# Causal scores of two batches as one step of 64-wide tile products, with the key halves of every second batch exchanged

## The chip, the cores and the metric

The kernel runs on one core of a Trainium2 chip. The metric is device time in microseconds (us), from the start of the launch to its end on that core. Where a profile is spoken of, it is one further execution, recorded by the hardware profiler; its times are counted from its first instruction.

The engines are named as the profile names them: PE (TensorE, matrix products; PEld is its loading of stationary operands), DVE (VectorE), ACT (ScalarE), POOL (GpSimd), and SP, whose queue issues all DMAs here.

## The reference, cut to what matters

An mLSTM cell (4 batches, 8 heads, 768 tokens, head size 40) is followed by a feed-forward layer with exact GELU (320 to 2048 to 320) on its 3072 output rows.

```python
for t in range(S):                               # one head of one batch
    m_new  = np.maximum(f[t] + m, i[t])
    f_stab, i_stab = np.exp(f[t] + m - m_new), np.exp(i[t] - m_new)
    C = f_stab * C + i_stab * np.outer(v[t], k[t])
    n = f_stab * n + i_stab * k[t]
    y[t] = sigmoid(o[t]) * (C @ q[t]) / np.maximum(np.abs(n @ q[t]), 1.0)
    m = m_new
x = y.transpose(0, 2, 1, 3).reshape(B * S, H * D)
out = gelu(x @ w_in) @ w_out
```

## The kernel before, in words

**Chunks.** The 768 tokens are cut into six chunks of 128 (c = 0 to 5). Within a chunk the recurrence is written as causal attention: scores k·q of 128 by 128 tokens for each head, times weights exp(a[s] − M[t]) that are zero where s comes after t, times the values with a column of ones. What comes from earlier chunks is q times a carried state. A chunk has four batches (b = 0 to 3). A **step** is one piece of this for one batch, and has a letter. The feed-forward layer of chunk c runs on the PE between the cell steps of chunk c + 1.

**The steps that matter here**, for c of 2 and more:

- `M` (`mask`, L381, POOL): the tile with M for all tokens t, sent to all 128 partitions by a DMA, gets a large number where s > t.
- `W` (`weights`, L407, ACT): eight exponentials, one for each head, with the column `aT[:, c, head]` (a of the token on each partition) as bias. Masked places become 0.
- `K` and `Q` (`turn_k`, `turn_q`, L430, DVE): k and q of one batch are turned to kT and qT, 64 partitions for each of two heads. `K` also forms `vw`, the values times `ewT` (L466, POOL).
- `S` (`scores`, L479, PE; L482, DVE): for each of four head pairs p and both heads of it (`hip`), the 64 by 128 slice of kT is the stationary operand and the 64 by 128 slice of qT is the moving one. The result is 128 tokens s by 128 tokens t. The two heads of a pair use the upper and the lower 64 rows of the PE array and write to two PSUM banks. Then DVE multiplies each bank (128x512) into the weights, in place. Nothing is saved for the masked triangle: 16 products of 128 columns for two batches.
- `C` (`carry_two`, two batches at once): q times state in 64 by 64 tiles of the PE array (L531), the new state's part from k and `vw` (L538, not in the last chunk), then DVE and POOL work on the results (L547, L554, L555).
- `V` (`values`, L573, PE): for each head and each half of the tokens t, weights times values, 128 rows by 64 columns of the array. DVE adds the carried part (L581).
- `F`: one of fourteen pieces of the down product (L844, 8 matmuls each). `Y`, `X`, `R` finish a batch and hand it to the feed-forward layer.

**Where the order comes from.** It is written out by hand, in the strings `FRONT` (chunks 0 and 1) and `DOWN` (later chunks); each engine executes its instructions in that order. The part of `DOWN` around the change reads as follows for a chunk, with `Z` empty except in chunk 2:

```
M0 Z M1 W0 F L3 F B3 W1 Z Z F S0 Z S1 K2 C0 M2 Z G0 G1 G2 G3 V0 Z V1 W2 Z F Q2 K3 Q3
Y0 M3 D3 F F W3 F Z S2 S3 C2 V2 V3 F ...
```

So on the PE a pair of batches is S, S, C, V, V, and then F; on DVE it is the products of both S, the turning `K2`, and then the results of C and V. `B3` sends M of the fourth batch by DMA (L162), after the sixteen small DMAs that `L3` issues for its k and q (L145); `M3` and `W3` can only run after it.

**PSUM.** S of an even batch takes two banks of pool `ps_mm` (tag "a"), S of an odd batch both banks of pool `ps_tr`. `V` uses tag "a" as well, `C` uses `ps_h`, `F` uses `ps_mm` tag "b".

Of the kernel before, what the change touches and what calls it, by code (L numbers as in the profile page):

```python
# [9 lines left out]
F32 = mybir.dt.float32  # L10
# [4 lines left out]
OP = mybir.AluOpType  # L15

P = 128
# [10 lines left out]
FRONT = """  # L28
    I2 O0 g0 L0 P0 L1 E k1 t0 P1 P2 k7 w0 N k2 w1 O1 K L2 Q s0 O3 w2 q D k2 d P3 t1 w3 c0 L3 J v0 t2 K K y0 s1 I7 v1
    I8 O2 J g1 L4 I5 c1 K I1 I2 y1 s2 x0 t3 B4 O4 B5 g2 J x1 s3 v2 c2 L5 y2 H T0 x2 G0 v3 g3 c3 K y3 M1 J L6 J A x3  # L30
    M0 K W0 O7 K A O6 O5 J M2 W1 S0 C0 K J J T1 U U K L7 V0 K T2 J J A G2 K G1 Y0 W2 S1 K M3 C1 A J S2 J K W3 K V1 C2
    Y1 T3 J J U U S3 V2 K K J G3 J Y2 C3 X0 K V3 J K F J F K K B8 F J K F F J K F F F R0 X1 J J K F J F K X2 F J K F
    J Y3 K F R1 J F Z B9 B10 F X3 R2 Z R3 F"""
DOWN = """
    M0 Z M1 W0 F L3 F B3 W1 Z Z F S0 Z S1 K2 C0 M2 Z G0 G1 G2 G3 V0 Z V1 W2 Z F Q2 K3 Q3 Y0 M3 D3 F F W3 F Z S2 S3
    C2 V2 V3 F N F Y1 X0 R0 Y2 F F Y3 X1 R1 F X2 R2 F X3 R3 F"""


# [1 line left out]
def kernel(  # L40
# [29 lines left out]
    R = P // 2  # L70
# [30 lines left out]
    aT = const.tile([P, NCH, BH], F32, name="aT")  # L101
    ewT = const.tile([P, NCH - 1, BH], F32, name="ewT")
# [9 lines left out]
    W = {n: shared([P, H, L], F32, f"W{n}") for n in range(B - 1)}  # L112
# [9 lines left out]
    f_sb = gates.tile([BH, NCH, L], F32, name="f_sb")  # L122
    i_sb = gates.tile([BH, NCH, L], F32, name="i_sb")
    M_d = dram.tile([NCH - 1, BH, L], F32, name="M_d")

    def out_of(n):
        return ob[n % NLD].rearrange("p (h d) -> p h d", d=D)

    def load(n, first=0, end=4):

        if n >= NCH * B:
            return
        c, b = divmod(n, B)
        for src, dst in ((q, qb), (k, kb), (v, vb), (o_gate, None))[first:end]:
            nc.sync.dma_start(out=dst[turn_of(n)][:, :, 0:D] if dst else out_of(n),  # L135
                              in_=src[b, :, c * L:(c + 1) * L, :].rearrange("h p d -> p h d"))

# [12 lines left out]
    def turn_of(n):  # L150

        return n % NLD if n < 2 * B else (n - 2 * B) % NQ
# [19 lines left out]
    for t in vb:  # L172
# [15 lines left out]
    a = gates.tile([BH, NCH, L], F32, name="a")  # L188
# [7 lines left out]
    for j in range(3):  # L196
        m = slice(BH * j, BH * (j + 1))
# [17 lines left out]
    def gates_turned(*parts):  # L215

        for src, dst in parts:
            n = dst.shape[1]
            pg = ps_tr.tile([P, n, BH], F32, name="pg", tag="tr")
            for c in range(n):  # L220
                nc.tensor.transpose(pg[:, c, :], src[:, c, :], ident[0:BH, 0:BH])
            nc.vector.tensor_copy(out=dst, in_=pg)

    def gates_of(c0, c1):

        flat = lambda t: t[:, c0:c1].rearrange("p c l -> p (c l)")
# [20 lines left out]
    def decays_turned(e0, e1, g0, g1):  # L247
        e, g = slice(e0, e1), slice(g0, g1)
        gates_turned((ew[:, e], ewT[:, e]), (gg[:, g], gT[:, g]))

    def decays_last(g0, g1):
        g = slice(g0, g1)
        pd = ps_tr.tile([P, g1 - g0, BH], F32, name="pd", tag="tr")
        nc.tensor.matmul(pd.rearrange("p c n -> p (c n)"), last, gT[:, g].rearrange("p c n -> p (c n)"),
                         start=True, stop=True)
        nc.vector.tensor_copy(out=dec[:, g], in_=pd)
# [92 lines left out]
            fetch(i + NB)  # L349


    halves = (slice(0, R), slice(R, P))

    idle = [0]

    def keep_clock(steps):
# [11 lines left out]
    class Cell:  # L368
# [9 lines left out]
        def mask(self, b):  # L378

            t = Mb[self.c * B + b]  # L380
            nc.gpsimd.affine_select(out=t, in_=t, compare_op=OP.is_ge, fill=1.0e30, base=0,  # L381
                                    pattern=[[0, H], [1, L]], channel_multiplier=-1)

        def weights(self, b):

# [83 lines left out]
        def scores(self, b):  # L469
            n = self.c * B + b  # L470
            kT, qT = self.kT.pop(b), self.qT[b]

            pool, tag = (ps_tr, "tr") if self.c > 0 and b % 2 else (ps_mm, "a")
            ps = [pool.tile([P, NP, L], F32, name="ps", tag=tag) for hip in range(2)]
            unread(ps[0][:, 0, :])
            for p in range(NP):
                for hip in range(2):
                    r = halves[hip]
                    nc.tensor.matmul(ps[hip][:, p, :], kT[r, p, :], qT[r, p, :], start=True, stop=True)  # L479
            for hip in range(2):  # L480
                w = W[n].rearrange("p (m two) t -> p m two t", two=2)[:, :, hip, :]
                nc.vector.tensor_tensor(out=w, in0=ps[hip], in1=w, op=OP.mult)  # L482

        def carry(self, b):

# [419 lines left out]
    def in_turn(steps):  # L905
        todo = list(steps)
        return lambda: todo.pop(0)() if todo else None

    def cell_steps(c, letters, before=None):
        cell = Cell(c)  # L910
        cell.before = before
        return dict(zip(letters, (cell.mask, cell.weights, cell.gate, cell.turn, cell.scores, cell.carry, cell.values,
                                  cell.finish, cell.turn_y, cell.split_x, cell.load_last, cell.turn_k,
                                  cell.turn_q, cell.weigh_last, cell.carry_two,
                                  cell.last_M)))

    first_g = Hidden(False)
    n_pieces = range(len(pieces))
    steps = dict(P=fetch, L=lambda n: load(n, 0, 2), O=lambda n: load(n, 2, 4), B=load_M, E=second_gates, N=later_gates,
                 I=keep_clock, k=warm, D=lambda: decays_turned(0, 2, 0, 1), Q=lambda: decays_turned(2, NCH - 1, 1, NCH - 1),  # L920
                 d=lambda: decays_last(0, 1), q=lambda: decays_last(1, NCH - 1),
                 A=in_turn(first_up_steps(0)), U=in_turn(first_up_steps(1)), F=in_turn(first_down_steps(first_g)),
                 K=in_turn(lambda i=i: conv_one(i) for i in n_pieces), H=products_begin,
                 J=in_turn(lambda i=i: conv_two(i) for i in n_pieces), Z=split_weight)
    steps |= cell_steps(0, "mwgtscvyx") | cell_steps(1, "MWGTSCVYXR")
    play(FRONT, steps)
    for c in range(1, NCH):
        g, later, steps = Hidden(True), [], {}
        if c + 1 < NCH:
            steps = cell_steps(c + 1, "MWGTScVYXRLKQDCB", g)  # L930
        up(g, weight_sum(1) + weight_sum(2) + weight_sum(3) if c == 1 else [], [lambda b=b: (steps["K"](b), steps["Q"](b)) for b in range(2)] if steps else [])
        if c == 1:
            later = weight_sum(4)
        products, late = down_steps(c, g)
        steps |= dict(F=in_turn(products), Z=in_turn(later), N=late)
        play(DOWN if c + 1 < NCH else "F " * 14, steps)
# [30 lines left out]
```

## Time and profile before

| | |
|---|---|
| median of 3 runs | 485.5 us (485.18 to 485.93) |
| the profiled execution's own time | 484.47 us |
| its span, first to last instruction | 482.7 us |
| PE clock granted in it | 1.00 |
| PE, share of the span that a matmul is in flight | 98% |
| DVE / ACT / POOL busy | 72% / 46% / 14% |
| L479, scores, 64x128 products | 384 records, first at 15.4 us, last at 400.1 us |
| L482, DVE products on 128x512 | 48 of them, 0.68 us each |

The program holds one matrix product as one instruction, and the trace shows two records for each fp32 product (both passes over the stationary operand): 16 products are "x32". A record's duration includes the way through the array, so records overlap; what a step costs is the distance between the starts of its first record and of the next step's first record. In the chain of waits the lines show these distances; there times are up to 0.1 us later than in the timeline, because the chain hands over at modelled ends.

### The profile page before, as it was taken

How to read it: one execution, taken by the hardware profiler on the slowest of the kernel's cores; microseconds unless marked ns; L12 is line 12 of the kernel's file. 1: busy time of each engine (PE TensorE's matmuls, PEld its weight loads, DVE VectorE, ACT ScalarE, POOL GpSimd, SP SyncE). 2: the span in 40 equal slices, each digit the busy share in tenths (PEclk: the TensorE clock that was granted, in tenths of full speed). 3: DMA queues.
4: the chain of work that ended last, by engine and by line, in shares of the span. 5: the costliest groups of instructions: out<-in, count | busy, mean ns of one | idle time of the engine just before them, and what ended most of it. 6: DMA issues, size and time to landing. Idle time of an engine off the chain costs nothing.

```text
span 482.7 us, 11369 instructions
## 1 busy us (share of the span) xinstructions
PE 473.8 (98%) x4484; PEld 413.6 (86%) x4484; DVE 346.4 (72%) x744; ACT 222.3 (46%) x477; POOL 69.5 (14%) x108
## 2 busy tenths in 40 slices
PE   7999999999999999999999999999999999999997
PEld 7788888877777999977999977999977899977997
DVE  7899699898979997747498757498857397724321
ACT  6977999844632941112951113961103852112300
POOL 3001200001000234200144200145000212000000
PEclk9999999999999999999999999999999999999999
DMA  9998955379320365921264922265921250100001
GB/s 174 202 220 180 208 145 140 90 184 218 104 27 7 36 126 76 206 50 22 31 117 72 216 50 25 29 127 75 205 49 22 32 90 3 47 9 0 1 1 54
DMA packets 168021, 44.28 MB, mean 92 GB/s; under 512 B 154176, under 2 KB 161504, under 8 KB 167968
## 3 DMA queue, kind: packets, MB, share of 16 engines
q1 hardware_dynamic: 167968, 43.56, 46.4%
q8 instruction: 35, 0.57, 0.5%
q14 instruction: 18, 0.15, 0.1%
HBM read 39.52 MB, written 4.01 MB: 90 GB/s over the span
## 4 chain that ended last, share of the span: by engine, by line
PE 91%; DVE 4%; SPq 1%; ACT 1%; DMA 1%; issue 1%; DVEq 0%
PE po L844 32%; PE pu L768 21%; PE po L821 7%; PE pu L713 6%; PE pu L779 6%; PE ph L573 5%; PE ps L479 5%; PE pf L531 2%; PE pu L719 2%; PE px L608 2%; PE pf L538 1%; SPq L135 1%; PE pt L453 1%; ACT g L783 1%; PE pf L498 1%; DMA ob<-in_o_gate_dram 1%
## 5 line engine op out<-in xcount | busy, mean ns | idle before, releaser
L844 PE MATMUL po<-w_out,g 128*128 128x160 f32 x640 | 91.2, 300 | 0.0
L844 PEld LDWEIGHTS po<-w_out,g 128*128 128x128 f32 x640 | 87.8, 190 | 1.8 <-ACT g L783 1.8
L783 ACT ACTIVATE g<-pu 128x512 f32<-128x512 f32 x80 | 40.8, 616 | 53.5 <-PE pu L779 53.3
L844 PE MATMUL po<-w_sums,sums 128*128 128x160 f32 x320 | 47.2, 302 | 0.0
L844 PEld LDWEIGHTS po<-w_sums,sums 128*128 128x128 f32 x320 | 44.2, 190 | 0.4
L618 ACT ACTIVATE x_hi<-px 128x384 fp32r<-128x384 f32 x20 | 9.8, 489 | 70.6 <-PE px L608 70.6
L768 PE MATMUL pu<-x_hi,w_in_hi 128*128 128x512 f32 x160 | 41.7, 402 | 0.0
L700 DVE TENSOR_TENSOR sums<-g 128x512 f32<-128x512 f32 x20 | 13.8, 689 | 38.6 <-ACT g L783 38.6
L768 PE MATMUL pu<-x_lo,w_in_lo 128*128 128x512 f32 x160 | 40.7, 396 | 0.0
L407 ACT ACTIVATE W<-W,aT 128x128 f32<-128x128 f32 x128 | 39.1, 389 | 0.4 <-POOL W L381 0.2
L482 DVE TENSOR_TENSOR W<-ps,W 128x512 f32<-128x512 f32 x40 | 25.5, 685 | 15.9 <-ACT W L407 10.9
L768 PEld LDWEIGHTS pu<-x_hi,w_in_hi 128*128 128x128 f32 x160 | 28.5, 188 | 9.4 <-ACT g L783 4.1
L768 PEld LDWEIGHTS pu<-x_lo,w_in_lo 128*128 128x128 f32 x160 | 30.1, 188 | 7.2
L821 PE MATMUL po<-w_out,g 128*128 128x320 f32 x128 | 35.3, 434 | 0.0
L857 DVE TENSOR_TENSOR o_sb<-po,o_sb 128x320 f32<-128x320 f32 (+1 forms) x27 | 12.6, 465 | 28.9 <-PE po L844 24.8
L821 PEld LDWEIGHTS po<-w_out,g 128*128 128x128 f32 x128 | 24.0, 190 | 9.8 <-DVE w_out L348 0.2
L768 PE MATMUL pu<-x_all,w_in_mid 128*128 128x512 f32 x80 | 31.7, 396 | 0.1
L783 ACT ACT_TABLE_LOAD x5 | 6.4, 1283 | 55.1 <-DMA blocks<-in_k_dram 27.5
L768 PE MATMUL pu<-x_all,w_mid 128*128 128x512 f32 x80 | 31.7, 396 | 0.0
L419 POOL MEMSET g<- 32x1024 f32 x8 | 7.6, 944 | 155.8 <-ACT W L407 155.6
L713 PE MATMUL pu<-first_x,w_in 128*128 128x256 f32 x128 | 28.9, 382 | 0.0
L381 POOL TENSOR_SCALAR_AFFINE_SELECT W<-W 128x1024 f32<-128x1024 f32 x16 | 18.1, 1137 | 67.3 <-DMA W<-M_d 58.9
(180 smaller groups left out, 907.8 us busy)
## 6 DMA issues: line engine op xcount, KB each, us to landing
W<-M_d SPq DMA_DIRECT2D x16, 512.0 KB, 5.7
bits<-in_moe_w_in_dram SPq DMA_DIRECT2D x20, 256.0 KB, 4.1
bits<-in_moe_w_out_dram SPq DMA_DIRECT2D x16, 320.0 KB, 3.6
ob<-in_o_gate_dram SPq DMA_DIRECT2D x24, 160.0 KB, 3.9
out_dram<-o_sb SPq DMA_DIRECT2D x24, 160.0 KB, 1.9
vb<-in_v_dram SPq DMA_DIRECT2D x22, 160.0 KB, 5.1
kb<-in_k_dram SPq DMA_DIRECT2D x22, 160.0 KB, 4.8
g<-M_d SPq DMA_DIRECT2D x4, 512.0 KB, 4.2
```

The costliest lines, as they stand in the source:

```text
L381: nc.gpsimd.affine_select(out=t, in_=t, compare_op=OP.is_ge, fill=1.0e30, base=0, pattern=[[0, H], [1, L]], channel_multiplier=-1)
L407: nc.scalar.activation(out=W[n][:, h, :], in_=src, func=AF.Exp, scale=-1.0, bias=aT[:, self.c, r:r + 1])
L479: nc.tensor.matmul(ps[hip][:, p, :], kT[r, p, :], qT[r, p, :], start=True, stop=True)
L482: nc.vector.tensor_tensor(out=w, in0=ps[hip], in1=w, op=OP.mult)
L573: nc.tensor.matmul(ph[r, h, :], Pm[:, h, r], vb[turn_of(n)][:, h, :], start=True, stop=True)
L700: nc.vector.tensor_tensor(out=s1, in0=a21, in1=a22, op=OP.add)
L713: nc.tensor.matmul(banks[-1][e][:, i - i0, :], in_tile(i, x)[:, e, i % 2 * P:(i % 2 + 1) * P], first_x[:, x, t0:t1], start=(x == 0 and i = ...
L768: nc.tensor.matmul(pus[i][e], w[k][:, e, i * P:(i + 1) * P], x[:, k, :], start=(n == 0 and k == 0), stop=False, skip_group_check=True)
L779: nc.tensor.matmul(pu[e], w[r, i // 2, i % 2 * P:(i % 2 + 1) * P], x[r, NX, :], start=False, stop=(n == 2), skip_group_check=True)
L783: nc.scalar.activation(out=g.t[:, HF * e + i, :], in_=pu[e], func=AF.Gelu, scale=4097.0)
L821: nc.tensor.matmul(po[b], g.t[:, f, b * L:(b + 1) * L], w_out[:, f, :], start=(f == 0), stop=(f == NF - 1))
L844: nc.tensor.matmul(bank[at][:, i, :], lhs(j, t), rhs(j), start=(first and i == 0 and j == 0), stop=(i == n - 1 and j == HF - 1), skip_grou ...
```

## The change

`S1` and `S3` are gone from `DOWN`, and `S` there is a new function `scores_two` for batches b and b + 1 (chunks 2 to 5; chunks 0 and 1 keep `scores`). It forms 64 by 64 tile products. The first half of the tokens s meets all 128 tokens t (x = 0); the second half of s meets only the second half of t (x = 1). The quarter with s in the second and t in the first half, all of it masked, is not computed. For one p and x, two batches and two heads make four products on four different quarters of the array. To give them four different quarters, the results of the odd batch stand in exchanged halves: its first 64 tokens s are on partitions 64 to 127.

All that is indexed by s must then be exchanged for batches 1 and 3 of chunks 2 to 5: k and v as loaded for `C` and `V` (two DMAs of 64 partitions in place of one of 128), the mask (two `affine_select`, of 64x1024 and 64x512, in place of one of 128x1024), and the columns of `aT` and `ewT`. Those are written to DRAM once (`r`, 2 DMAs, in the middle of `FRONT`) and read back exchanged (`p`, 4 DMAs, at its end). DVE multiplies each bank in two parts: the columns t of the second half on all partitions, and those of the first half on 64 partitions.

```diff
-    M0 Z M1 W0 F L3 F B3 W1 Z Z F S0 Z S1 K2 C0 M2 Z G0 G1 G2 G3 V0 Z V1 W2 Z F Q2 K3 Q3 Y0 M3 D3 F F W3 F Z S2 S3
+    M0 Z M1 W0 F L3 F B3 W1 Z Z F S0 Z K2 C0 M2 Z G0 G1 G2 G3 V0 Z V1 W2 Z F Q2 K3 Q3 Y0 M3 D3 F F W3 F Z S2
...
+    def swapped(c, b):
+
+        return c > 1 and b % 2 == 1
...
+            if dst and swapped(c, b):
+                x, to = src[b, :, c * L:(c + 1) * L, :].rearrange("h p d -> p h d"), dst[turn_of(n)][:, :, 0:D]
+                for i in range(2):
+                    nc.sync.dma_start(out=to[halves[i]], in_=x[halves[1 - i]])
+                continue
...
+    def halves_out():
+
+        for t, t_d in zip((aT, ewT), swapped_d):
+            nc.sync.dma_start(out=t_d, in_=t[:, 2:])
+
+    def halves_back():
+
+        for t, t_d in zip((aT, ewT), swapped_d):
+            to, by = [x.rearrange("p c (b h) -> p (c b) h", h=H)[:, 1::2] for x in (t[:, 2:], t_d)]
+            for i in range(2):
+                nc.sync.dma_start(out=to[halves[i]], in_=by[halves[1 - i]])
...
-            nc.gpsimd.affine_select(out=t, in_=t, compare_op=OP.is_ge, fill=1.0e30, base=0,
-                                    pattern=[[0, H], [1, L]], channel_multiplier=-1)
+            for x, base in ((t[0:R], -R), (t[R:P, :, 0:R], 0)) if swapped(self.c, b) else ((t, 0),):
+                nc.gpsimd.affine_select(out=x, in_=x, compare_op=OP.is_ge, fill=1.0e30, base=base,
+                                        pattern=[[0, H], [1, x.shape[2]]], channel_multiplier=-1)
...
+        def scores_two(self, b0):
+
+            two_b = (b0, b0 + 1)
+            ps = [[pool.tile([P, NP, L], F32, name="ps", tag=tag) for hip in range(2)] for pool, tag in ((ps_mm, "a"), (ps_tr, "tr"))]
+            kT, qT = [self.kT.pop(b) for b in two_b], [self.qT[b] for b in two_b]
+            for p in range(NP):
+                for x in range(2):
+                    t = slice(R * x, P)
+                    for i in range(2):
+                        for hip in range(2):
+                            r = halves[hip]
+                            nc.tensor.matmul(ps[i][hip][halves[x ^ i], p, t], kT[i][r, p, halves[x]], qT[i][r, p, t],
+                                             start=True, stop=True)
+            for i, b in enumerate(two_b):
+                for hip in range(2):
+                    w = W[self.c * B + b].rearrange("p (m two) t -> p m two t", two=2)[:, :, hip, :]
+                    for r, t in ((slice(0, P), halves[1]), (halves[i], halves[0])):
+                        nc.vector.tensor_tensor(out=w[r, :, t], in0=ps[i][hip][r, :, t], in1=w[r, :, t], op=OP.mult)
```

More of the change, by code (lines that the diff above doesn't have):

```diff
@@ L30 @@
     I8 O2 J g1 L4 I5 c1 K I1 I2 y1 s2 x0 t3 B4 O4 B5 g2 J x1 s3 v2 c2 L5 y2 H T0 x2 G0 v3 g3 c3 K y3 M1 J L6 J A x3
-    M0 K W0 O7 K A O6 O5 J M2 W1 S0 C0 K J J T1 U U K L7 V0 K T2 J J A G2 K G1 Y0 W2 S1 K M3 C1 A J S2 J K W3 K V1 C2
+    M0 K W0 O7 K A O6 O5 J M2 W1 S0 C0 K J J T1 U U K L7 V0 K T2 r J J A G2 K G1 Y0 W2 S1 K M3 C1 A J S2 J K W3 K V1 C2
     Y1 T3 J J U U S3 V2 K K J G3 J Y2 C3 X0 K V3 J K F J F K K B8 F J K F F J K F F F R0 X1 J J K F J F K X2 F J K F
-    J Y3 K F R1 J F Z B9 B10 F X3 R2 Z R3 F"""
+    J Y3 K F R1 J F Z B9 B10 F X3 R2 Z R3 F p"""
 DOWN = """
-    M0 Z M1 W0 F L3 F B3 W1 Z Z F S0 Z S1 K2 C0 M2 Z G0 G1 G2 G3 V0 Z V1 W2 Z F Q2 K3 Q3 Y0 M3 D3 F F W3 F Z S2 S3
+    M0 Z M1 W0 F L3 F B3 W1 Z Z F S0 Z K2 C0 M2 Z G0 G1 G2 G3 V0 Z V1 W2 Z F Q2 K3 Q3 Y0 M3 D3 F F W3 F Z S2
     C2 V2 V3 F N F Y1 X0 R0 Y2 F F Y3 X1 R1 F X2 R2 F X3 R3 F"""
@@ L124 @@
     M_d = dram.tile([NCH - 1, BH, L], F32, name="M_d")
+    swapped_d = [dram.tile([P, n, BH], F32, name=f"swapped{n}") for n in (NCH - 2, NCH - 3)]
     def out_of(n):
         return ob[n % NLD].rearrange("p (h d) -> p h d", d=D)
+    halves = (slice(0, R), slice(R, P))
+    def swapped(c, b):
+        return c > 1 and b % 2 == 1
     def load(n, first=0, end=4):
@@ L349, in conv_two @@
             fetch(i + NB)
-    halves = (slice(0, R), slice(R, P))
     idle = [0]
@@ L914, in cell_steps @@
                                   cell.turn_q, cell.weigh_last, cell.carry_two,
-                                  cell.last_M)))
+                                  cell.last_M, cell.scores_two)))
     first_g = Hidden(False)
@@ L920 @@
                  I=keep_clock, k=warm, D=lambda: decays_turned(0, 2, 0, 1), Q=lambda: decays_turned(2, NCH - 1, 1, NCH - 1),
-                 d=lambda: decays_last(0, 1), q=lambda: decays_last(1, NCH - 1),
+                 d=lambda: decays_last(0, 1), q=lambda: decays_last(1, NCH - 1), r=halves_out, p=halves_back,
                  A=in_turn(first_up_steps(0)), U=in_turn(first_up_steps(1)), F=in_turn(first_down_steps(first_g)),
@@ L929 @@
         if c + 1 < NCH:
-            steps = cell_steps(c + 1, "MWGTScVYXRLKQDCB", g)
+            steps = cell_steps(c + 1, "MWGTscVYXRLKQDCBS", g)
         up(g, weight_sum(1) + weight_sum(2) + weight_sum(3) if c == 1 else [], [lambda b=b: (steps["K"](b), steps["Q"](b)) for b in range(2)] if steps else [])
```

## The prediction

> **What bounds the kernel now.** First the page's busy times, then its chain of waits. Their lines:
>
> ```profile
> PE 473.8 (98%) x4484; PEld 413.6 (86%) x4484; DVE 346.4 (72%) x744; ACT 222.3 (46%) x477; POOL 69.5 (14%) x108
> ...
> PE 91%; DVE 4%; SPq 1%; ACT 1%; DMA 1%; issue 1%; DVEq 0%
> ```
>
> PE sets the end, so a shorter PE step pays, but only if what waits behind it is ready. So I read the stage itself: the chain for the first pair of batches of chunk 3 and of chunk 5, then the DVE timeline of both.
>
> ```profile
> 238.66 1.99 PE ps L479 x32
> 240.64 1.07 PE pf L531 x64
> 241.71 1.06 PE pf L538 x32
> 242.78 1.87 PE ph L573 x64
> ...
> 384.50 1.99 PE ps L479 x32
> 386.49 1.07 PE pf L531 x64
> 387.56 2.00 PE ph L573 x64
> ```
> ```profile
> 239.88 2.49 DVE L482 TENSOR_TENSOR W<-ps,W 128x512 f32<-128x512 f32 x4 [2.84 <-ACT W L407]
> 242.28 1.41 DVE L430 STREAM_TRANSPOSE kT<-blocks 64x512 f32<-64x512 f32 x2
> ...
> 385.72 2.48 DVE L482 TENSOR_TENSOR W<-ps,W 128x512 f32<-128x512 f32 x4 [2.84 <-ACT W L407]
> 388.12 1.41 DVE L430 STREAM_TRANSPOSE kT<-blocks 64x512 f32<-64x512 f32 x2
> ```
>
> S, C, V follow each other on PE without a gap. From the start of S: F follows at 5.99 us in chunk 3 (1.99 + 1.07 + 1.06 + 1.87), at 5.05 us in chunk 5, which has no L538 (384.43 to 389.48). DVE starts 1.3 us after S does, since the even batch's scores are done half-way, and ends its four products about 3.8 us after the start (242.37). V of the odd batch starts near 4.95 us in chunk 3, 4.0 us in chunk 5. DVE's lead is 1.1 us there, 0.2 us here. That lead is the subject.
>
> The third place is the second pair of chunk 2:
>
> ```profile
> 178.86 1.09 POOL L381 TENSOR_SCALAR_AFFINE_SELECT g<-g 128x1024 f32<-128x1024 f32 x1 [4.95 <-DMA g<-M_d]
> 179.99 2.45 ACT L407 ACTIVATE g<-g,aT 128x128 f32<-128x128 f32 x8 [2.17 <-POOL g L381]
> ```
>
> S starts at 179.42; the last batch's weights are ready at 182.44, and DVE's products of it wait for that. This goes back to a DMA, not to PE.
>
> **What the Trainium skill says.** "TensorEngine Tiling (Array Packing)", Key Properties: tiles operate independently, changing the tiling mode drains the engine. The trace agrees: records of L531 start in groups of four, 7 ns apart, one group every 58 ns; from L479's last record to L531's first are 0.20 us. The same page, PSUM Bottleneck: tiling speeds up TensorE but not the emptying of PSUM, which may become the bottleneck. No run here shows that yet; it is my forecast. "TensorE: Matmul & The Clock Gate", Part 3, Measured speedup: sixteen tiles gave 10.6 times; for our four tiles the trace proves only about 2 (below). "SBUF — State Buffer", Who interferes with whom: a GpSimd instruction and a VectorE copy or tensor_scalar block each other. The trace agrees: L588 takes 0.66 us beside the POOL mask at 251.99, 0.17 us alone.
>
> **The change, part by part.**
>
> *PE, scores.* Down products give the price of a record: 128 columns of weights against 320 take 272 ns (17.43 us / 64), against 160 139 ns (8.89 / 64), so 0.83 ns a column and 5.5 ns. 128 columns: 112 ns, which is the spacing of L479's pairs of records. 64 columns: 59 ns, also the floor that L531 and L573 show with 41 columns. Four tiles at once: each head pair costs two passes of 112 and two of 59 ns, 0.34 us; four pairs 1.36, and about 0.09 for the first weights. Both S and C then use 64x64 tiles, so I drop the 0.20 us drain. D, from S to C, is 1.45 us for 1.99. The gain on PE is 0.54 x 8 = 4.3 us if nothing waits. Bounds: 1.40 without first-load cost; at worst 2.5, if four tiles stream no faster than L531 proves: 64 records in 1.07 us are 16.7 ns each against 34 ns of streaming, 2.05 at once; 32 records of 107 ns and 32 of 53 ns are 5.1 us / 2.05.
>
> *DVE, scores.* For two batches, 4 products of 512 columns become 8 of 256. Four of 512 run in 2.49 us, the last 0.68: a step of 0.60 to 0.62. Four of 164 (L547) run in 1.03, a step of 0.24 to 0.26. So 1.04 ns a column and 0.087: 0.354 for 256, the last 0.416. Eight: 2.90 us for 2.49. They no longer start half-way: every bank is completed by the last head pair. Start: last record (D − 0.06) + its 0.24 + 0.10 that DVE took after L479 (254.62 to 254.72) = D + 0.26. V of the odd batch needs all eight for its second head: D + 0.26 + 7 x 0.354 + 0.416 + 0.054 (from a DVE end to L573 at 26.99) = D + 3.21; its seven heads of 0.117 and the switch to L844 are 0.94. F follows at **D + 4.15 = 5.60 us**. PE alone would give D + 4.0 with L538, D + 3.06 without.
>
> So a pair gains 0.39 in chunks 2 to 4 and loses 0.55 in chunk 5: there the DVE products, before just hidden behind C, become the wait. What queues behind V on PE is F.
>
> *Second pairs.* DVE's later work moves back by 4.59 − 3.70 = 0.89 us (start of K2). In chunk 3 it was idle only 0.30 us before the second S's products; S comes 0.39 earlier and its products are ready 0.5 later; some 0.2 us remain as a wait. Chunk 4 had 0.86 idle: nothing. Chunk 2: its mask is now two instructions of 1.09 and about 0.64 (0.29 at 128 columns, 1.10 at 1024), so weights at 183.08, products of the odd batch till 184.6, F at 185.6 without the 0.90 us gap that the chain shows inside V at 184.83. That gap has no semaphore; I keep it: 186.5 for 186.56.
>
> *The rest, at nothing.* Masks M1: POOL is 14% busy, M1 is made a stage ahead; uncovered 0.64 each. Split loads of k and v: each SP issue takes about 0.5 us, they stand after the M of B3, and vw of chunk 3's fourth batch is ready at 254.4, 2.7 us before L538 needs it; late by 1 us it still is in time. The sixteen small loads and the M behind `L3` pass no new DMA in their chunk. `r` stands ahead of the w_out loads: two issues, about 1 us of SP, while `bits` has four buffers; uncovered 1 us, once. `p` falls into SP's idle time (129.8 to 136.4) and lands long before W1 of chunk 2 (163.95); its 1,792 packets at 21 ns over 16 engines are an estimated 2.4 us. aT is read only by later instructions.
>
> *Sum.* Chunk 2: −0.05. Chunk 3: −0.39 − 0.39 + 0.2 = −0.58. Chunk 4: −0.78. Chunk 5: +0.55 x 2 = +1.10. Together −0.3 us: 484.47, the profiled execution's own time, becomes 484.2; against the median of 485.5, one us above it, **485.2**.
>
> **The rivals.**
>
> *Slower, by DVE.* Place: the eight products before V. If halves of rows of a bank do not overlap as L547 does, a step costs its full 0.416: 7 x 0.062 = 0.43 us more in each pair but chunk 2's (7 pairs, 3.0 us): 488.2. From a step of 0.36 us on the change costs time, from 0.38 measurably. For it: DVE is at 88% in these stages. Against: L547 with a PSUM input and a broken pattern overlaps.
>
> *Slower, by PE.* Four tiles give only 2.05 streams: D = 2.5, F at 6.65; 0.66 x 5 pairs and 1.6 x 2, about +7: 492. Against: two tiles run at full rate both ways (L479 in rows, L503 in columns).
>
> *Faster.* D = 1.40, the gap of 0.90 does not return, and the mask's two parts cost no more than one: the sum's −0.3, then −0.05 x 6, −0.9 and −0.6 are −2.1: 483.4, between 483.1 and 484.2.
>
> *It doesn't do what it says.* S needs both kT at once and four banks free. DVE ends chunk 3's turning at 251.96, S starts at 253.46: 1.5 us, of which the 0.89 and 0.39 take most. If it falls short: +0.3 in each of seven pairs, 487.
>
> **How the numbers follow.** What a measurement of this kernel can tell from no change is about 0.2%, 1 us. Forecast, waits of V eat the gain: 0.52, own range 484.2 to 486.6, of which 0.05 lies below 484.5 and 0.05 above 486.5. Faster: 0.15. DVE: 0.19. PE: 0.09. Banks or kT: 0.05. So faster 0.15 + 0.05 = 0.20; within, 0.42; slower 0.33 + 0.05 = 0.38. The range 484.0 to 489.0 reaches over the DVE rival and leaves out PE's and about half of the faster one.
>
> **What would show it.** In the changed kernel's line numbers S is L518 and L524, C L573, V L615. L518 to L573 in 1.4 to 1.5 us, records in fours 112 and 59 ns apart: the PE step. L524 x8 in about 2.9 us, starting 1.7 us after S. L615 cut by a wait for DVE W, most of all in chunk 5, where F follows at 5.6 us. Busy PE falling by 4 us with the span unchanged: the forecast as a whole. I am wrong if V shows no wait, if D is above 1.7, or if anything before 160 us moves.

## The result, and the profile after

| | before | after |
|---|---|---|
| median, 13 runs each on one chip | 485.03 us (484.26 to 486.21) | 487.64 us (486.06 to 493.69) |
| ratio of the runs | 1 | 1.0060, 95% interval 1.0038 to 1.0082 |
| the profiled execution's own time, its span | 484.47, 482.7 us | 487.46, 485.6 us |

The change made the kernel slower by 0.6%, some 2.6 us; no change within 0.2% had been forecast. In 4 of the 13 runs with the change the mean granted clock lay below 0.998, and these are longer (488.7 to 493.7 us; the longest is left out of the ratio); without such runs the medians are 487.1 us with the change and 484.7 before (on the chip of e1), and the main experiments below keep their order (e7 482.7, e4 484.1, e5 484.7, e1 485.5, e10 485.7, e9 487.1).

First the page of the changed kernel, the busy times and the shares of the chain:

```profile
PE 472.1 (97%) x4740; PEld 411.4 (85%) x4740; DVE 350.0 (72%) x776; ACT 222.3 (46%) x477; POOL 76.9 (16%) x116
...
PE 68%; DVE 12%; SPq 5%; DMA 5%; ACT 5%; issue 3%; POOL 2%; DVEq 0%; ACTq 0%; POOLq 0%
```

PE is busy 1.7 us less in a span 2.9 us longer; 4 us less in an unchanged span had been forecast. It was 91% of the chain and is 68%. What it now waits for stands in the waits of PE (total us, how often, longest):

```profile
PE ph L615 <- DVE W L524: 1.9, 5, 0.5
PE ph L615 <- DMA blocks<-in_k_dram: 1.4, 1, 1.4
PE ph L615 <- DVE g L524: 1.1, 3, 0.5
...
PE px L650 <- DVE y_rest L639: 0.9, 1, 0.9
```

Three kinds: V (L615) for DVE's products, eight times; V once for what is put down to a DMA; and the last transposes X (L650) for DVE. Each in the timeline (start, duration, engine and line). For V, the first pair of chunk 5:

```profile
385.85 1.57 PE L518 MATMUL ps<-qT,kT 64*64 64x128 f32 x64
...
387.24 1.09 PE L573 MATMUL pf<-state,qT 64*64 64x41 f32 x64
387.55 3.10 DVE L524 TENSOR_TENSOR W<-ps,W 128x256 f32<-128x256 f32 x8 [3.25 <-PE ps L518]
...
389.10 1.17 PE L615 MATMUL ph<-vb,W 128*64 128x41 f32 x32 [0.28 <-DVE W L524]
...
390.79 1.02 PE L615 MATMUL ph<-vb,W 128*64 128x41 f32 x28 [0.52 <-DVE W L524]
391.73 0.43 PEld L886 LDWEIGHTS po<-w_sums,sums 128*128 128x128 f32 x3
391.74 0.54 PE L886 MATMUL po<-w_sums,sums 128*128 128x160 f32 x2
```

S to C is 1.39 us. DVE's eight end 4.79 us after S, V's second head goes on at 4.94, and F follows at 5.88. Chunk 3's second pair, V of its two batches, and chunk 4's end (DVE's finishing chain, the masks of chunk 5 on POOL, and X):

```profile
256.38 1.11 PE L615 MATMUL ph<-vb,W 128*64 128x41 f32 x32
...
258.86 1.14 PE L615 MATMUL ph<-vb,g 128*64 128x41 f32 x32 [1.37 <-DMA blocks<-in_k_dram]
```
```profile
336.12 2.08 POOL L404 TENSOR_SCALAR_AFFINE_SELECT W<-W 128x1024 f32<-128x1024 f32 x1
337.17 2.10 DVE L916 TENSOR_TENSOR g<-g,sums 128x1024 f32<-128x1024 f32 x1
...
342.27 0.49 DVE L633 TENSOR_TENSOR ob<-ob,den 128x320 f32<-128x320 f32 x1
...
343.54 1.95 POOL L404 TENSOR_SCALAR_AFFINE_SELECT W<-W 64x1024 f32<-64x1024 f32 x2 [5.34 <-DMA W<-M_d]
343.78 1.19 DVE L633 TENSOR_TENSOR ob<-ob,den 128x320 f32<-128x320 f32 x1
...
344.89 0.68 DVE L639 COPY y_rest<-ob 128x128 f32<-128x128 f32 x1
...
345.62 0.33 PE L650 MATMUL px<-ident,y_rest 128*128 128x128 f32 x1 [0.92 <-DVE y_rest L639]
```

In the first, V of the odd batch starts 1.1 us after DVE has ended (257.78), so it is not DVE's products that it waits for. In the second, L633 and L639 take 1.19 and 0.68 us beside the masks, 0.49 and 0.23 elsewhere; F follows X after 1.47 us, before after 0.39.

The third place that the prediction read, chunk 2's second pair:

```profile
177.14 1.81 POOL L404 TENSOR_SCALAR_AFFINE_SELECT g<-g 64x1024 f32<-64x1024 f32 x2 [1.03 <-DMA g<-M_d]
...
178.98 2.45 ACT L430 ACTIVATE g<-g,aT 128x128 f32<-128x128 f32 x8 [1.32 <-POOL g L404]
```

The two-part mask takes 1.81 us for 1.09, but the weights are ready at 181.43, before DVE needs them (183.36).

A stage is counted from the first up product of one chunk to that of the next; the cell steps of one chunk lie in it. Us in the profiles:

| stage of chunk | before | after | difference | forecast |
|---|---|---|---|---|
| 2 | 74.56 | 74.47 | −0.09 | −0.05 |
| 3 | 72.90 | 73.72 | +0.82 | −0.58 |
| 4 | 72.95 | 73.90 | +0.95 | −0.78 |
| 5 | 71.03 | 72.65 | +1.62 | +1.10 |

### The profile page after: what moved, and what is told of

Its sections match the earlier page's. It is cut to its first block, busy times and chain, and to the rows that moved or that the text cites. A ratio compares the mean times of both kernels' runs of the same rounds, so it can differ in the third digit from the quotient of the medians.

```text
span 485.6 us, 12001 instructions
## 1 busy us (share of the span) xinstructions
PE 472.1 (97%) x4740; PEld 411.4 (85%) x4740; DVE 350.0 (72%) x776; ACT 222.3 (46%) x477; POOL 76.9 (16%) x116
## 4 chain that ended last, share of the span: by engine, by line
PE 68%; DVE 12%; SPq 5%; DMA 5%; ACT 5%; issue 3%; POOL 2%; DVEq 0%; ACTq 0%; POOLq 0%
PE pu L810 21%; PE po L886 19%; PE po L863 7%; PE pu L755 6%; PE pu L821 5%; SPq L157 4%; PE ph L615 3%; ACT g L825 2%; PE pu L761 2%; POOL g L442 2%; PE px L650 2%; DVE qT L453 1%; DMA g<-in_q_dram 1%; DVE W L524 1%; DVE kT L453 1%
## 5 line engine op out<-in xcount | busy, mean ns | idle before, releaser
L404 POOL TENSOR_SCALAR_AFFINE_SELECT W<-W 128x1024 f32<-128x1024 f32 (+2 forms) x20 | 21.8, 1098 | 62.7 <-DMA W<-M_d 40.6
L524 DVE TENSOR_TENSOR W<-ps,W 128x256 f32<-128x256 f32 (+1 forms) x48 | 17.7, 414 | 12.7 <-PE ps L518 12.3
```

Source lines behind the costliest of these rows:

```text
L404: nc.gpsimd.affine_select(out=x, in_=x, compare_op=OP.is_ge, fill=1.0e30, base=base, pattern=[[0, H], [1, x.shape[2]]], channel_multiplier=-1)
L524: nc.vector.tensor_tensor(out=w[r, :, t], in0=ps[i][hip][r, :, t], in1=w[r, :, t], op=OP.mult)
```

## The experiments

Theory A: DVE's products are dearer than forecast and V waits for them. Two further theories belong to the other waits: D, PE waits for its own instructions; F, masks on POOL hold up DVE. Ratios are to the kernel before on the same chip; differences between kernels are taken between medians (the kernel before has 484.7 to 485.0 us on every chip used). The length of a gap or wait of PE is its idle time, as the profile gives it.

### e1_order: DVE's odd products in another order

```diff
-                for hip in range(2):
-                    w = W[self.c * B + b].rearrange("p (m two) t -> p m two t", two=2)[:, :, hip, :]
-                    for r, t in ((slice(0, P), halves[1]), (halves[i], halves[0])):
-                        nc.vector.tensor_tensor(out=w[r, :, t], in0=ps[i][hip][r, :, t], in1=w[r, :, t], op=OP.mult)
+                ws = [W[self.c * B + b].rearrange("p (m two) t -> p m two t", two=2)[:, :, hip, :] for hip in range(2)]
+                parts_of = ((slice(0, P), halves[1]), (halves[i], halves[0]))
+                todo = [(hip, x) for hip in range(2) for x in parts_of] if i == 0 else [(hip, x) for x in parts_of for hip in range(2)]
+                for hip, (r, t) in todo:
+                    w = ws[hip]
+                    nc.vector.tensor_tensor(out=w[r, :, t], in0=ps[i][hip][r, :, t], in1=w[r, :, t], op=OP.mult)
```

> The odd batch's four DVE products in the order 128 rows, 128 rows, 64 rows, 64 rows (before: 128, 64, 128, 64). Theory A, an instruction that begins on another partition than the one ahead of it does not overlap it: the steps of the odd batch become 0.33 (last of the even batch to first 128), 0.33, 0.44 to 0.46, 0.33 us instead of 0.33, 0.44, 0.46, 0.44; the eight end 0.23 us sooner after S (4.55 for 4.79), V of the odd batch and F follow 0.23 sooner (F at 5.65 for 5.88 us in chunk 5); with at most seven pairs the time falls by 0.9 to 1.6 us, to about 486.3. Rival B, the odd batch's products wait for more semaphores, or C, the PSUM banks of its pool are slower to read: its steps stay at 0.44 to 0.46 us in any order and the time stays at 487.6.

485.99 us, ratio 1.0027 (1.0010 to 1.0045): 1.6 us less than the change. The timeline of chunk 4's second pair, changed kernel and then this one; in each the even batch's four products (`W`) and the odd one's (`g`):

```profile
328.50 1.41 DVE L524 TENSOR_TENSOR W<-ps,W 128x256 f32<-128x256 f32 x4 [0.38 <-PE ps L518]
...
329.83 1.76 DVE L524 TENSOR_TENSOR g<-ps,g 128x256 f32<-128x256 f32 x4
```
```profile
330.62 1.41 DVE L526 TENSOR_TENSOR W<-ps,W 128x256 f32<-128x256 f32 x4 [0.63 <-PE ps L518]
...
331.96 1.53 DVE L526 TENSOR_TENSOR g<-ps,g 128x256 f32<-128x256 f32 x4
```

The starts within the odd batch are 0.44, 0.46, 0.44 us apart in the changed kernel, 0.33, 0.435, 0.348 here: only the step from 128 rows (from partition 0 on) to 64 rows (from partition 64 on) stays long. F follows S at 5.63 to 5.66 us for 5.86 to 5.89, in the pairs of chunks 3 to 5 without a wait of another kind. The waits and the banks are the same in both orders, so B and C fall and A holds.

### e2_fetch: 32 PE instructions more at the start

```diff
-    warm(6)
+    warm(4)
+    warm_narrow(10)
```

`warm_narrow` is `warm` with products of one column.

> 32 more PE instructions (20 records of one column's product and their weight loads, less two wide warming products) within the first 7 us, where PE waits; nothing else. Theory D, the 1.38 us gap of PE ahead of V of chunk 3's second odd batch is a wait for PE's own instructions, which come in blocks of 256: the block's border now lies 32 instructions earlier in the program, so that gap moves to the even batch's V or the end of the new-state part (about 3.6 us after S instead of 5.6), the border's PE index stays 5313 (193 modulo 256), and chunk 2's and 4's first pairs get a gap at the same place; no gap of V of the odd batch is then longer than 0.75 us. The time changes by less than 1.5 us either way, as such gaps stand in for the wait on DVE. Rival E, the gap is a wait on a semaphore (DVE's additions into the state, or the last load of k and v): it stays at V of the odd batch, 1.4 us long, 5.8 us after S.

Chunk 3's second pair, V of the even batch, which is now cut in two:

```profile
257.66 0.65 PE L621 MATMUL ph<-vb,W 128*64 128x41 f32 x16
259.35 0.61 PE L621 MATMUL ph<-vb,W 128*64 128x41 f32 x15 [1.04 <-issue]
```

The gap moved from the odd batch's V to the middle of the even one's, with PE's index 5313 (its place in PE's instructions, counted as told below) as before; chunk 2's went into the new-state part (0.71 us, index 3009). Chunk 4's first pair got none, against the expectation. For theory D speaks more: PE's 9,593 instructions on record, 9,480 matmuls and weight loads and its waits for semaphores, fill 37 blocks of 256, and the trace has 37 fetches of 16,384 bytes on an instruction queue (before: 9,042, 35 blocks, 35 fetches). Counting these instructions in order of time, each of these gaps stands at an index that leaves 193 when divided by 256, and ends 1.2 to 1.5 us after such a fetch does:

```
kernel   place             index  border passed  fetch            PE goes on
before   chunk 2, 2nd pair  3521   181.56        182.78-184.24    185.73
after    chunk 2, 1st pair  3009   165.22        166.09-167.33    168.67
after    chunk 3, 2nd pair  5313   254.41        256.05-257.38    258.64
after    chunk 4, 1st pair  6337   312.64        313.50-314.43    315.72
e1       chunk 3, 2nd pair  5313   253.88        256.09-257.47    258.93
e2       chunk 3, 2nd pair  5313   255.36        256.62-257.96    259.35
```

So the 0.90 us gap of the kernel before that the prediction could give no cause was one of these too. E, a semaphore, falls: it would not have moved. The time, 490.28 us (1.0141, 1.0089 to 1.0193), missed its expectation. Part comes from the start: PE's granted clock was 0.79 between 8 and 16 us and chunk 2's S came 1.3 us later, probably for the two wide warming products fewer, since all four runs have a mean clock of 0.996 or less. The rest goes with the clock too: the two runs at 0.996 took 488.2 and 488.5 us, those at 0.993 and 0.990 took 492.1 and 495.0. What lowered it in these two is not shown.

### e3_mask: one mask instruction for the exchanged batches

```diff
-            for x, base in ((t[0:R], -R), (t[R:P, :, 0:R], 0)) if swapped(self.c, b) else ((t, 0),):
+            for x, base in ((t, 0),):
```

> The masks of the exchanged batches as one instruction of 128x1024, as for the others; the mask then stands at the wrong tokens, so the weights of these batches are other ones. Theory F, chunk 4's wait at the last transposes (X to F 1.47 us for 0.39) comes from the second mask instruction running on POOL beside DVE's L633 and L639: without it these take 0.49 to 0.60 and 0.23 us instead of 1.19 and 0.68, and the last X of chunk 4 is followed by F after 0.4 to 0.7 us; the time falls by 0.6 to 1.5 us, to about 486.6. Rival G, DVE is merely late there because the scores' products grew: L633 stays long, or the wait stays with short instructions; the time stays within 0.3 us of 487.6.

488.20 us, 1.0065 (1.0039 to 1.0091): no gain. The end of chunk 4:

```profile
343.02 1.09 POOL L404 TENSOR_SCALAR_AFFINE_SELECT W<-W 128x1024 f32<-128x1024 f32 x1 [4.72 <-DMA W<-M_d]
343.19 0.95 DVE L630 TENSOR_SCALAR den<-qb 128x8 f32<-128x8 f32 x1
...
344.68 0.49 DVE L633 TENSOR_TENSOR ob<-ob,den 128x320 f32<-128x320 f32 x1
```

L633 is short again, but the one mask now stands beside L630 (0.95 us for 0.16), and X waits 0.55 us (0.92 changed). F as stated, that the second instruction does it, falls; that masks do it stays open until e13.

### e4_hide and e7_order_hide: F between C and V

```diff
-    M0 Z M1 W0 F L3 F B3 W1 Z Z F S0 Z K2 C0 M2 Z G0 G1 G2 G3 V0 Z V1 W2 Z F Q2 K3 Q3 Y0 M3 D3 F F W3 F Z S2
-    C2 V2 V3 F N F Y1 X0 R0 Y2 F F Y3 X1 R1 F X2 R2 F X3 R3 F"""
+    M0 Z M1 W0 F L3 F B3 W1 Z Z F S0 Z K2 C0 M2 Z G0 G1 G2 G3 F V0 Z V1 W2 Z Q2 K3 Q3 Y0 M3 D3 F F W3 F Z S2
+    C2 F V2 V3 N F Y1 X0 R0 Y2 F F Y3 X1 R1 F X2 R2 F X3 R3 F"""
```

> One piece F of the down product moved from behind V to between C and V in both pairs of every chunk. Theory A, what V waits for is DVE's eight products, which end 4.8 us after S while PE alone needs V's second head at 4.4 (chunks 2 to 4) or 3.4 (chunk 5): with 2.3 us of other PE work in between, the wait of V goes: the last V of a pair ends 1.39 + 1.03 + 1.06 + 2.3 + 1.9 = 7.7 us after S (6.6 in chunk 5), against 5.88 + 2.3 = 8.2 before: 0.5 us in six pairs and up to 1.6 in chunk 5's two: 3 to 5 us, so 483 to 485. Rival H, DVE has no time left in these stages and its work only shifts: V no longer waits, but the second S waits for its transposes (DVE) by as much as was gained in each first pair, and the gain is only that of the second pairs, 1 to 2 us: 486.

> Both edits that helped: the odd batch's products as 128, 128, 64, 64 rows, and F between C and V. Theory A: V's wait is gone already with F ahead of it, so the 0.22 us that the order saves a pair is worth something only where DVE is late afterwards (the transposes ahead of the second S, the last transposes of chunk 4): at most 0.2 us a chunk, 0.3 to 0.8 in all, 483.5. Rival: DVE is the bound of the first half of each stage, and each pair gains the whole 0.22: 1.5 us, 482.5.

e4: 484.07 us, 0.9977 (0.9955 to 0.9999). e7, with e1's order as well: 482.70 us, 0.9958 (0.9943 to 0.9973), 2.3 us less than before and 4.9 less than the change. Chunk 4's second pair in e4:

```profile
329.95 2.44 PE L886 MATMUL po<-w_sums,sums 128*128 128x160 f32 x16
...
332.32 1.13 PE L615 MATMUL ph<-vb,W 128*64 128x41 f32 x32
...
333.28 1.11 PE L615 MATMUL ph<-vb,g 128*64 128x41 f32 x32
```

V no longer waits; in most pairs its last record comes 7.68 us after S (6.62 in chunk 5), as A had it. The stages of e7 are 73.67, 72.26, 73.93, 70.13 us: all but chunk 4's below those of before. There PE waits 0.72 us at X, the third kind of wait. e7 gained 1.4 us on e4, near the rival's 1.5, but not in the rival's way: in the profiles the pairs of chunks 3 to 5 take as long in both (7.84 us from S to the F after V, 8.56 in chunk 4's first pair, 6.78 in chunk 5), and the 1.4 us lie in the stage of chunk 2 (75.08 and 73.67). There, in the second pair, e4's S takes 0.65 us longer, waiting for qT, and PE waits 0.55 us more at index 3521. That the order of DVE's products brings this about is not shown.

### e5_full and e10_full_hide: the whole squares

```diff
-                    t = slice(R * x, P)
+                    t = slice(0, P)
...
-                    for r, t in ((slice(0, P), halves[1]), (halves[i], halves[0])):
-                        nc.vector.tensor_tensor(out=w[r, :, t], in0=ps[i][hip][r, :, t], in1=w[r, :, t], op=OP.mult)
+                    nc.vector.tensor_tensor(out=w, in0=ps[i][hip], in1=w, op=OP.mult)
```

> The triangle is not left out: both halves of s meet all 128 tokens t, in the same exchanged 64 by 64 tiles, and DVE multiplies each whole bank in one product of 128x512 (four a pair). S becomes 16 passes of 112 ns, about 1.85 us for 1.39; DVE's four take 2.49 us for 3.09 and start 0.31 us after S. Theory A (the wait of V is set by S plus DVE's products): DVE ends 4.65 us after S for 4.79, V of the odd batch and F follow 0.1 us sooner (F at 5.75 to 5.85), so the time is that of the change within 0.5 us, 487.2: what the left-out triangle saves on PE is paid back by DVE's shorter and more numerous products. Rival, PE is still the bound: each of eight pairs is 0.46 us longer, 3.7 in all, 491.

> Both: the whole squares with four DVE products a pair (as in the run that did not leave the triangle out), and F between C and V. Theory A: with the wait of V gone, S's length counts in full: 1.80 us for 1.39 in eight pairs, 3.3 us more than with the triangle left out, 0.5 to 1 of it given back by DVE's shorter work (2.49 us a pair for 2.87 to 3.09): about 485 against 482.7 (products reordered) and 484.1 (not). Rival: DVE's load decides here too, and the version with whole banks is as fast as the others or faster: 483 or less.

| | V after C | F between C and V |
|---|---|---|
| whole squares, four DVE products | e5: 485.00, 1.0007 (0.9990 to 1.0024) | e10: 485.97, 1.0021 (1.0005 to 1.0038) |
| triangle left out, eight DVE products | the change: 487.64, 1.0060 (1.0038 to 1.0082) | e4: 484.07, 0.9977 (0.9955 to 0.9999) |

S is 1.80 us for 1.39 in e5, yet F follows sooner: at 5.75 us in the first pairs of chunks 3 and 4 (5.89 and 5.98 changed), at 5.56 to 5.59 in chunk 5 (5.86 to 5.88). Leaving the triangle out costs 2.6 us with V after C, and gains 1.9 with F in between. Not all of the 2.6 is V's wait for DVE's products, which is worth 0.14 us in a pair of chunk 3 and 0.3 in one of chunk 5: e5 came out 2.2 us below its expectation because the stage of chunk 2 (73.43 us for 74.47) and the waits for blocks (0.53 for 1.37 in chunk 3) and at X (0.27 for 0.92) were shorter too. e10 lies 1 us above its own.

### e6_keep: the old scores in the last chunk

```diff
-        return c > 1 and b % 2 == 1
+        return 1 < c < NCH - 1 and b % 2 == 1
```

> The last chunk alone has the scores of before (S, S with products of 128x512, tokens not exchanged); chunks 2 to 4 are as changed. Theory A: chunk 5 has no new-state part on PE, so its pairs go back from 5.88 to 5.05 us, 1.66 us in all, and the time to about 486.0. Rival: most of the loss lies in chunks 2 to 4 (the blocks of PE instructions, DVE behind at chunk 4's last transposes) and chunk 5 only inherits it: F at 5.05 there again, but less than 0.6 us of the time.

485.79 us, 1.0010 (0.9995 to 1.0025), 1.85 less than the change. Chunk 5's stage is 71.01 us (72.65 changed, 71.03 before). Its first pair:

```profile
386.10 2.48 DVE L506 TENSOR_TENSOR W<-ps,W 128x512 f32<-128x512 f32 x4 [2.84 <-ACT W L431]
...
387.87 2.07 PE L616 MATMUL ph<-vb,W 128*64 128x41 f32 x64
...
389.86 2.44 PE L887 MATMUL po<-w_sums,sums 128*128 128x160 f32 x16
```

V runs through, and F is back at 5.05 us. A holds for this chunk, in place and size.

### e8_best: e7 with 16 PE instructions fewer

```diff
-    warm(6)
+    warm(2)
```

> As the run before it, with four wide warming products fewer in the first 7 us: 16 PE instructions fewer ahead of everything. Theory D (PE waits at the border of a block of 256 instructions where it has passed 256 in less than some 4 us): with F between C and V the trace of that version has waits of 0.78 and 0.64 us at the indices 3521 and 6337; a border 16 instructions later in the program meets pairs in which the last 290 instructions took 4.35 us or more, so both waits go, and no gap of over 0.4 us at an index of 193 modulo 256 is left between 160 and 420 us: about 1 us less than the run before, 482.5. Rival E (the waits are set by other engines): gaps and time as in the run before, within 0.3 us.

488.79 us, 1.0073 (1.0044 to 1.0102): a miss of 6 us. The gap at 6337 went; that at 3521 stayed, 2.9 us long: PE had passed the 256 instructions before it in 2.66 us, where the expectation had 4.35 or more, and the fetch began 3.10 us after the border. What followed, by windows of 3 us (start and end; length; busy us of PE, PEld, DVE, ACT, POOL; PE's granted clock; DMA):

```profile
187.00:190.00 3.00, 3.00 (x24) 2.92 (x23) 2.00 (x7) 0.00 (x0) 0.00 (x0) 0.50 0.30 27
190.00:193.00 3.00, 3.00 (x32) 2.67 (x32) 0.49 (x1) 0.00 (x0) 0.00 (x0) 0.61 0.37 41
```

From 185.5 us on, within the gap, PE's clock is granted at half for 6.8 us. e1's profile has half the clock for 3.4 us after its gap of 2.2 us (0.72 and 0.71 in the windows from 259 to 262 and from 262 to 265 us); after 1.8 us in e3 it stays 1.00. A long gap is not needed for it, though: the profiles of e2, e5 and e10 have 3.4 us at half the clock from 8.0, 15.5 and 15.3 us on, with no gap over 1.2 us ahead of that. In e8 the start has one too (0.60 from 9 to 12 us), and chunk 2's S comes 1.4 us later than in e7. All six runs of e8 have a mean clock of 0.997 or less, none of e7's six, so the missing products are the likely reason for it. Why the fetch began so late is open.

### e9_before_hide: F moved in the kernel before

```diff
-    M0 Z M1 W0 F L3 F B3 W1 Z Z F S0 Z S1 K2 C0 M2 Z G0 G1 G2 G3 V0 Z V1 W2 Z F Q2 K3 Q3 Y0 M3 D3 F F W3 F Z S2 S3
-    C2 V2 V3 F N F Y1 X0 R0 Y2 F F Y3 X1 R1 F X2 R2 F X3 R3 F"""
+    M0 Z M1 W0 F L3 F B3 W1 Z Z F S0 Z S1 K2 C0 M2 Z G0 G1 G2 G3 F V0 Z V1 W2 Z Q2 K3 Q3 Y0 M3 D3 F F W3 F Z S2 S3
+    C2 F V2 V3 N F Y1 X0 R0 Y2 F F Y3 X1 R1 F X2 R2 F X3 R3 F"""
```

> The kernel before, with F between C and V in both pairs of chunks 2 to 5 as in the two fastest versions; the scores stay as they were. Theory A: V waits there for nothing in chunks 3 to 5 (its only long gap in the profile is one of 1.1 us in chunk 2), so there is nothing to hide: the time stays within 0.6 us of 485.0, and what the fastest version gains comes from the shorter S. Rival: moving F is what helps, whatever the scores: it falls by 1.5 us or more, towards 482.7.

487.24 us, 1.0044 (1.0020 to 1.0068): slower, which neither had expected. Moving F costs 2.5 us with the old scores, and the new scores cost 2.6 with F in its old place; only both together, in e4 and e7, gain. Against before, the stages of chunks 2 to 5 differ by −0.49, +2.09, +1.01 and +0.38 us. Part of this is the move itself: in chunk 3's first pair, S, C, V and one piece F take 8.49 us for 8.26. Most of chunk 3's loss is the third kind of wait, at its end (F 1.78 us after X for 0.33):

```profile
270.15 2.38 POOL L381 TENSOR_SCALAR_AFFINE_SELECT W<-W 128x1024 f32<-128x1024 f32 x2
...
271.51 1.11 DVE L597 COPY y_rest<-ob 128x128 f32<-128x128 f32 x1
...
272.67 0.33 PE L608 MATMUL px<-ident,y_rest 128*128 128x128 f32 x1 [1.24 <-DVE y_rest L597]
```

### e11_rest: y_rest copied by ACT, on e7

```diff
-            nc.vector.tensor_copy(out=y_rest, in_=ob[(self.c * B + b) % NLD][:, NX * P:].unsqueeze(1).to_broadcast([P, 2, R]))
+            (nc.scalar.copy if self.c > 1 else nc.vector.tensor_copy)(out=y_rest, in_=ob[(self.c * B + b) % NLD][:, NX * P:].unsqueeze(1).to_broadcast([P, 2, R]))
```

> The fastest version so far, with the copy into y_rest (0.22 us, four a chunk) on ACT in place of DVE in chunks 2 to 5. If chunk 4's wait at the last transposes (0.99 us in that version's trace) is DVE being late there, it falls by 0.2 to 0.7 us and the time by 0.2 to 1 us, to about 482.2; if what is late is only the mask's overlap with one instruction, it stays at 0.8 to 1 us and the time within 0.2 us.

484.17 us, 0.9987 (0.9972 to 1.0002): 1.5 us above e7, unexpected. Chunk 4's wait fell from 0.72 to 0.39 us, but chunk 3 got one of 1.19: POOL's masks began 1.5 us before DVE's last L635 and held up two instructions ahead of it.

### e12_loads: without later loads of k and v

```diff
+            if dst and c > 2:
+                continue
```

> The changed kernel without the loads of k and v for chunks 3 to 5 (kb and vb keep the values of chunk 2; the outputs of these chunks are other ones): some 0.64 MB less to move in each stage, and about sixteen DMA issues fewer on SP. Theory D, PE waits for its own instructions behind the kernel's data on the DMA queues: ahead of V of chunk 3's second odd batch the block of 16,384 bytes is under way within 1 us of the border (1.64 us in the changed kernel), and the gap at PE index 5313 falls from 1.38 (0.75 to 2.2 in other runs of the same code there) to the 0.6 us that DVE's products cause alone, so F follows S there after 5.88 us for 6.92; in time 0.5 to 1.5 us, to about 486.5. Chunk 5's pairs, which load nothing, stay at 5.88. Rival: the block comes late whatever the queues carry: the gap stays at 0.75 or more and the time at 487.6.

In chunk 3's second pair the gap at index 5313 is 0.26 us and F follows at 5.92 us for 6.92: as expected there. The fetch began 1.23 us after the border (1.64 changed) and took 0.92 (1.33). The time went the other way, to 489.84 us, 1.0102 (1.0080 to 1.0123): with the loads gone, M arrives earlier, the masks run earlier (from 267.73 us on in chunk 3, for 271.27), L635 takes 1.02 us beside them in place of 0.49, and X waits 0.96, 0.96 and 0.69 us in chunks 2, 3 and 4.

### e13_nomask: without chunk 5's masks

```diff
+            if self.c == NCH - 1:
+                return
```

> The changed kernel without the four masks of chunk 5 (its weights keep the later tokens; two of these masks run on POOL while chunk 4 is being finished). Theory F, widened: chunk 4's wait at the last transposes is the time by which masks on POOL hold up DVE's finishing chain (L916 2.10 us beside a mask for 1.21, L633 1.19 for 0.49, L639 0.68 for 0.23: 2.0 us in all). Without them these take 1.21, 0.49 and 0.23 us, no gap of PE over 0.4 us is left at the last transposes of chunk 4, and F follows X after 0.4 us for 1.47: 1.0 us of the time, about 486.6. Theory G, DVE is late there by its own work (the scores' products take 0.6 us a pair more): the gap stays at 0.8 us or more though L916, L633 and L639 are short, and the time within 0.3 us of 487.6.

486.55 us, 1.0045 (1.0029 to 1.0061), 1.1 less than the change. The end of chunk 4:

```profile
343.31 0.49 DVE L635 TENSOR_TENSOR ob<-ob,den 128x320 f32<-128x320 f32 x1
343.72 0.22 DVE L641 COPY y_rest<-ob 128x128 f32<-128x128 f32 x1
...
344.95 0.27 PE L652 MATMUL px<-ident,y_rest 128*128 128x128 f32 x1
```

The wait is gone and the stage is 72.65 us for 73.90; chunk 3's stage is the same to 0.01. F in its wider form holds, G falls: DVE has the time, unless a mask takes it.

## Why the prediction was wrong, step by step

**PE's step was right.** D is 1.39 us for 1.45, in fours 109 to 112 and 56 to 58 ns apart, without a drain. Four 64 by 64 tiles at once run at full rate: the rival with D = 2.5 is out.

**The step that failed** is DVE's: "Eight: 2.90 us", a step of 0.354 for all. The even batch's steps are 0.33, better than that; the odd batch's are 0.44, 0.46 and 0.44, for each of them starts on another partition than the one ahead of it. The eight take 3.10 us and start 0.05 later, V follows their end after 0.15 us for 0.054, and the end of the chain, "F follows at D + 4.15", is D + 4.50: 5.88 us for 5.60. e1 took 0.22 of these 0.28 us away by the order alone. The trace of before had the number, in rows that stand side by side:

```profile
243.72 0.56 DVE L547 TENSOR_TENSOR far<-pf,gT 128x164 f32<-128x164 f32 x2
244.20 0.65 DVE L555 TENSOR_TENSOR state<-state,pf 64x164 f32<-64x164 f32 x2
```

L547's pairs, both from partition 0 on, start 0.25 us apart, but L555's, partitions 0 to 63 and then 64 to 127, start 0.32 to 0.34 apart at the same 164 columns. The prediction priced half a bank by L547, where L555 was the nearer row. Its rival "Slower, by DVE" named place and price: with 0.43 more a pair it gave 488.2; the runs gave 0.28 and 487.6. That the times are so near is in part chance, for waits that the rival did not have make up the difference.

**Where the rest came from.** The sum per stage closes with three terms (us, from the profiles):

| chunk | forecast | DVE's step | PE's instructions | masks at X | other | sum | measured |
|---|---|---|---|---|---|---|---|
| 3 | −0.58 | 2 x 0.28 | 1.04 | | −0.20 | +0.82 | +0.82 |
| 4 | −0.78 | 2 x 0.28 | 0.10 | 1.08 | | +0.96 | +0.95 |
| 5 | +1.10 | 2 x 0.28 | | | | +1.66 | +1.62 |

The −0.20 is the DVE backlog that was put on chunk 3's second pair and did not come. In chunk 2 the terms nearly cancel, and that −0.09 came near the forecast −0.05 is chance: the first pair lost 0.11, in the second the 0.90 us gap did not return, the weights were ready 1.65 us earlier than forecast (181.43 for 183.08), and S waited for qT from DVE. Of the 3.6 us between forecast and measured, DVE's step makes 1.7, and the two terms that the prediction put at nothing make 2.2. The whole is +2.9 us of span, with 0.25 gained ahead of 130 us, where only the two writes `r` were added; the prediction had counted any such move against itself, and its cause is open.

**"The rest, at nothing"** did not hold. The Trainium skill, "Runtime: NRT & Kernel Launch", Instruction fetch mechanics, says that instructions come in 16 KiB blocks of 256 and that crossing a border is mostly hidden. The trace agrees on the blocks. The crossing was not always hidden: in the 15 traces, between 140 and 430 us, PE stopped at 28 borders by over 0.35 us from one start to the next, each time after it had passed the 256 instructions before in 2.6 to 3.1 us and where the fetch had begun 0.2 to 3.1 us after the border before. Where the fetch began ahead of that border, as for 3521 and 6849 in the changed kernel (256 instructions in 2.62 and 2.83 us), PE did not stop. The change puts 448 PE instructions (S, C and V) into the 5.9 us of a pair where there were 384, and no term stood for them. And the masks were costed at their own 0.64 us, uncovered, not at what they do to DVE: "SBUF — State Buffer", Who interferes with whom, which the prediction cites, says that a VectorE instruction with two SBUF inputs contends with a GpSimd one that reads SBUF. L916 and L633 have two, and took 2.10 and 1.19 us beside a mask for 1.21 and 0.49. What decides there seems to be less the mask's length (e3) than when it runs (e9, e11, e12).

**What stays open.** The waits for blocks and at X move with edits that have nothing to do with them; what sets the moment at which a fetch begins is not shown (in e12 it came earlier with less traffic, at one border). What brings the half clock on is not shown either, and e2 and e8 have no run without it, so what their edits cost apart from the clock is not known. In e9 some 0.2 us a stage stay unexplained.

## What to carry to other kernels

When a step on the bounding engine is halved, price the engine that empties it by the nearest row in form, start partition and all, and put other work between the two: the left-out triangle cost 2.6 us with V behind it, other waits included, and gained 1.9 with F in between; but the move of F alone cost 2.5. Order an engine's instructions so that neighbours start on the same partition. Where the bounding engine's instructions get more and shorter, count them against the blocks of 256 in which they are fetched, and look for what else runs beside the last chain ahead of a stage's end.

## What the runs showed of the hardware that was not expected

- DVE instructions with an operand in PSUM overlap their neighbour by 0.07 us (0.33 us apart at 0.406 long) when both start on the same partition, and do not (0.435 to 0.46 apart) when the start changes between 0 and 64.
- Where PE stopped at the border of a block of 256 instructions, it went on 1.2 to 1.7 us after a fetch of 16,384 bytes had ended; the fetch took 0.9 to 1.5 us and began up to 3.1 us after the border before.
- The granted clock fell to half for 3.4 us with a PE gap of 2.2 us ahead of it (e1), and for 6.8 us with one of 2.9 (e8). The Trainium skill, "TensorE: Matmul & The Clock Gate", Part 1, has the half clock follow an idle window of about 3.4 us; here the gaps were shorter, and in e2, e5 and e10 none over 1.2 us stood ahead of it, so the traces give no least gap.
